# One halving of the key products on VectorE ahead of the identity matmuls, in a cached-attention decode kernel on Trainium2

## The chip, the cores and the metric

The kernel runs on one core of one Trainium2 chip. Its engines have an instruction stream each: TensorE (PE in the profile; PEld is its loading of the stationary operand), VectorE (DVE), ScalarE (ACT), GpSimd (POOL) and SyncE (SP), whose queue issues nearly all loads here. TensorE writes to PSUM; the other data lie in SBUF, 128 partitions wide. The metric is the device time of one execution in microseconds, the median of the runs.

## The reference

One token goes through a layer that mixes cached attention (32 heads, 65,536 cached keys and values of 128 numbers each, bf16) with a small gated feed-forward part.

```python
q = (x @ wq).reshape(B, Sq, H, Dh).transpose(0, 2, 1, 3)      # B = Sq = 1, H = 32, Dh = 128
scores = jnp.einsum("bhqd,bhkd->bhqk", q, k_cache) * (Dh ** -0.5)   # Sk = 65536
p = jax.nn.softmax(scores, axis=-1)
o = jnp.einsum("bhqk,bhkd->bhqd", p, v_cache)
a = o.transpose(0, 2, 1, 3).reshape(B, Sq, H * Dh) @ wo       # D = 512
b = (silu(x @ w_gate) * (x @ w_up)) @ w_down                  # F = 1792
g = sigmoid((x * gate_w).sum(-1, keepdims=True))
out = g * a + (1 - g) * b
```

The two caches are 32 x 65,536 x 128 bf16 each, some 537 MB; every byte is read once.

## The kernel before

A head's 65,536 keys are cut into CH = 4 chunks of 128 partitions x KPP = 128 keys, so there are N = 128 chunks in all. A chunk of keys, and one of values, fills one slot: 128 partitions x 16,384 bf16, 4 MB. There are SLOTS = 5 slots, used in turn by every tile that `slot()` hands out: the weights wq first, then key and value chunks in the order k0, k1, v0, k2, v1, k3, v2 and so on, and wo, the gate and up weights, and the down weights near the end. A load can be issued when the tile that had its slot five places earlier is no longer needed. All these loads go through SyncE's queue in that order (`load`, L111), so a load that waits for its slot holds those behind it. In steady state a value load of chunk n takes the slot of the keys of chunk n - 1, and a key load of chunk n that of the values of chunk n - 4.

The work on one chunk n goes in two halves of HK = 64 keys per partition:

- `products` (L163): VectorE multiplies the half's keys by q, in place. q lies in `q_bc`, the same on all partitions, and is read again for each of the 64 keys.
- `sums` (L178): TensorE adds up each key's 128 products. The identity is the stationary operand, so a matmul copies its moving operand, 64 keys x 8 of the 128 products, into one PSUM bank `S_ps`, and 16 matmuls in a row accumulate: 8 partial sums are left for each key.
- `gather` (L188): VectorE reduces these 8 to one score; after the second half ScalarE takes the exponential of all 128 scores (L193) into `P_sb` and adds up the row.
- `pv` (L216): TensorE multiplies with the values of the chunk before, 32 matmuls per chunk, 16 in each half, into `O_ps`, which gathers over a head's four chunks.

At a head's end `O_ps` is copied by ScalarE (L228), `diagonal` picks the diagonal blocks with tiny matmuls (L238), and ScalarE copies the result to `o_all` (L243). Before chunk 125 VectorE has three small operations (L251, L254, L346) that normalise the first 31 heads. At the end stand the projection of these heads (L320), the feed-forward part (L278 to L315), the values of the last two chunks and the last head's ending.

The program is written in this order, but the order on each engine is made by a scheduler when the program is built. On VectorE it came out as product, product, reduce, reduce for each chunk, where the second reduce of a chunk comes before the first product of the next. On TensorE it came out as 16 + 13 matmuls of L178, 16 of L216, the last 3 of L178, and 16 of L216. Engines wait for one another on semaphores; the waits that matter are those of L178 for the product (VectorE), of L188 for the last matmul of its half (TensorE), of L163 for the key load, and of the loads for the slot's last reader.

## Time and profile before

| what | value |
|---|---|
| median of 3 runs | 2546.85 us (2546.82 to 2547.63) |
| the profiled execution, its time | 2547.63 us |
| its span, first to last instruction | 2545.9 us |
| mean granted TensorE clock | 0.909 |
| HBM read | 1087.64 MB, 427 GB/s over the span |
| TensorE, identity matmuls (L178) | 4096, 437 ns each in the mean |
| TensorE, value matmuls (L216) | 4064, 379 ns each in the mean |
| VectorE, products (L163) | 254 long ones, 4421 ns each; 4 half as long, 2293 ns |
| VectorE, reduces (L188) | 256, 691 ns each |
| key load, issue to landing (median) | 37.9 us |
| value load, issue to landing (median) | 31.7 us |

The page shows busy times and shares by engine first, then the span in 40 slices of 63.6 us, where each digit is a busy share in tenths. A group's row reads: line, engine, operation, what it writes <- what it reads, count | total busy us, mean ns of one | idle time of the engine just before, and what ended it. The duration of a matmul is longer than its distance to the next one, since matmuls are pipelined. The granted clock is the share of TensorE's full clock that was allowed. In the timeline a row is a start, a length, the engine, line and operation, a count where several were merged, and in brackets the idle time before it with what ended it. A row of the waits says who waited for whom, with the total, the number of times and the longest.

### The profile page before, as it was taken

To read this page: it belongs to the slowest core of one execution; us is meant where nothing else is said; L and a number is where in the kernel's file an instruction comes from. 1 tells how busy PE (TensorE), PEld (TensorE's weight loads), DVE (VectorE), ACT (ScalarE), POOL (GpSimd) and SP (SyncE) were. 2 spreads that over 40 slices of the span, in tenths; PEclk is the share of its full clock that TensorE was granted. 3 is DMA by queue.
4 is the path that set the end of the run, shared out by engine and by line. 5 is a ranking of instruction groups with operands and counts; after the bars stand their busy time and mean duration, and the time that the engine had idled before them with its cause. 6 is when DMAs were issued, how large, how long until landed. Compare 5 with 4: busy or idle time off the path is not lost.

```text
span 2545.9 us, 19309 instructions
## 1 busy us (share of the span) xinstructions
PE 2085.1 (82%) x8741; PEld 811.0 (32%) x8742; DVE 1302.3 (51%) x535; ACT 82.1 (3%) x330; POOL 1.0 (0%) x8
## 2 busy tenths in 40 slices
PE   6888888788878877888888887878887888788878
PEld 2333333333333333333333332333333333233334
DVE  4445544554455455545554554455445545554552
ACT  1000000000000000000000000000000000000000
POOL 0000000000000000000000000000000000000000
PEclk8988898998998899999898899899899889999988
DMA  9999999999999999999999999999999999999998
GB/s 404 432 429 432 431 430 432 429 432 432 430 432 431 431 430 432 430 432 432 430 433 429 432 431 432 431 431 430 431 431 431 433 430 430 433 429 433 430 429 324
DMA packets 43416, 1088.88 MB, mean 428 GB/s; under 512 B 4291, under 2 KB 8390, under 8 KB 9670
## 3 DMA queue, kind: packets, MB, share of 16 engines
q1 hardware_dynamic: 43332, 1087.65, 99.6%
q8 instruction: 68, 1.11, 0.2%
q14 instruction: 14, 0.11, 0.0%
q10 hardware_dynamic: 2, 0.00, 0.0%
HBM read 1087.64 MB, written 0.00 MB: 427 GB/s over the span
## 4 chain that ended last, share of the span: by engine, by line
DMA 64%; PE 26%; DVE 9%; SPq 0%; issue 0%; ACT 0%; DVEq 0%
DMA slot<-in_A_k_cache_dram 63%; PE S_ps L178 13%; PE O_ps L216 12%; DVE slot L163 9%; DMA slot<-in_A_v_cache_dram 1%; SPq L263 0%; PE c_ps L206 0%; SPq L111 0%; PE c_ps L238 0%; ACT O_sb L228 0%; SPq L117 0%; PE tot_ps L247 0%; DVE out_sb L360 0%; SPq L98 0%; PE a_ps L320 0%
## 5 line engine op out<-in xcount | busy, mean ns | idle before, releaser
L178 PE MATMUL S_ps<-slot,ident 128*128 128x512 bf16 x4096 | 1127.5, 437 | 424.9 <-DVE slot L163 424.9
L163 DVE TENSOR_TENSOR slot<-slot,q_bc 128x8192 bf16<-128x8192 bf16 (+1 forms) x258 | 1121.7, 4388 | 251.8 <-DMA slot<-in_A_k_cache_dram 244.4
L216 PE MATMUL O_ps<-slot,P_sb 128*4 128x512 bf16 x4064 | 918.0, 379 | 1.2 <-DMA slot<-in_A_v_cache_dram 1.2
L178 PEld LDWEIGHTS <-ident 128*128 128x128 bf16 x4096 | 437.7, 109 | 1096.6 <-issue 772.7
L188 DVE TENSOR_REDUCE S_sb<-S_ps 128x64 f32<-128x512 f32 x256 | 176.9, 691 | 951.2 <-PE S_ps L178 951.2
L216 PEld LDWEIGHTS <-P_sb 128*4 128x4 bf16 x4064 | 324.2, 85 | 574.2 <-issue 108.3
L193 ACT ACTIVATE P_sb<-S_sb 128x128 bf16<-128x128 f32 x128 | 39.6, 309 | 2309.0 <-DVE S_sb L188 2309.0
L238 PE MATMUL c_ps<-pick,O_sb 4*128 4x1 f32 x256 | 33.5, 248 | 21.6 <-ACT O_sb L228 21.6
L238 PEld LDWEIGHTS c_ps<-pick,O_sb 4*128 4x128 f32 x256 | 30.8, 186 | 37.8 <-ACT O_sb L228 37.8
L193 ACT ACTIVATION_READ_ACCUMULATOR P_sb<-S_sb 128x1 f32 x128 | 23.9, 186 | 0.0
L228 ACT ACTIVATE O_sb<-O_ps 4x512 f32<-4x512 f32 x32 | 18.8, 586 | 87.0 <-PE O_ps L216 87.0
L137 PE MATMUL q_ps<-slot,X_bc 128*128 128x512 bf16 x31 | 8.5, 431 | 6.3 <-DMA slot<-in_A_wq_dram 6.3
L320 PE MATMUL a_ps<-slot,oT 128*1 128x512 bf16 x32 | 7.4, 385 | 0.3 <-DVE oT L356 0.3
L137 PEld LDWEIGHTS <-X_bc 128*128 128x128 bf16 x32 | 3.4, 108 | 11.2 <-issue 6.7
L278 PEld LDWEIGHTS <-slot 128*128 128x128 bf16 x112 | 6.8, 161 | 0.4 <-issue 0.4
L278 PE MATMUL gu_ps<-X_bc,slot 128*128 128x1 bf16 x112 | 6.9, 198 | 0.0
L286 DVE COPY gu_sb<-gu_ps 128x28 f32<-128x28 f32 x1 | 0.2, 186 | 12.9 <-PE gu_ps L278 12.9
L243 ACT ACTIVATE o_all<-c_ps 128x1 f32<-128x1 f32 x31 | 5.3, 171 | 35.3 <-PE c_ps L238 35.3
L297 PE MATMUL b_ps<-slot,hT 128*1 128x512 bf16 x14 | 4.8, 515 | 1.4 <-DVE hT L294 1.4
L144 ACT ACTIVATE q_bc<-q_ps 128x512 bf16<-128x512 f32 x8 | 4.8, 597 | 9.8 <-PE q_ps L137 9.8
L251 DVE TENSOR_REDUCE tot_10469<-tot_ps 128x1 f32<-128x4 f32 x1 | 0.2, 161 | 9.5 <-PE tot_ps L247 9.5
L320 PEld LDWEIGHTS <-oT 128*1 128x1 bf16 x32 | 2.6, 84 | 4.6 <-issue 0.4
(37 smaller groups left out, 19.2 us busy)
## 6 DMA issues: line engine op xcount, KB each, us to landing
slot<-in_A_k_cache_dram SPq DMA_DIRECT2D x127, 4096.0 KB, 37.9
slot<-in_A_v_cache_dram SPq DMA_DIRECT2D x127, 4096.0 KB, 31.7
slot<-in_A_k_cache_dram SPq DMA_DIRECT2D x4, 1024.0 KB, 11.2
slot<-in_A_wo_dram SPq DMA_DIRECT2D x1, 4096.0 KB, 29.7
slot<-in_A_wq_dram SPq DMA_DIRECT2D x1, 3072.0 KB, 21.2
slot<-in_A_v_cache_dram SPq DMA_DIRECT2D x1, 2048.0 KB, 25.8
slot<-in_B_w_gate_dram SPq DMA_DIRECT2D x1, 1792.0 KB
slot<-in_B_w_up_dram SPq DMA_DIRECT2D x1, 1792.0 KB, 14.4
```

Source lines behind the costliest of these rows:

```text
L137: nc.tensor.matmul(q_ps, lhsT=X_bc[:, t, :], rhs=wq_sb[:, t, g * QG : (g + 1) * QG], start=(t == 0), stop=(t == KT - 1),)
L144: nc.scalar.activation(out=q_bc[:, g * QG : (g + 1) * QG], in_=q_ps, func=ACT.Copy)
L163: nc.vector.tensor_tensor(out=w, in0=w, in1=q_rep, op=ALU.mult)
L178: nc.tensor.matmul(t, lhsT=ident, rhs=w[:, :, s * R : (s + 1) * R], start=(s == 0), stop=(s == steps - 1),)
L188: nc.vector.tensor_reduce(out=S_sb[n][:, i * HK : (i + 1) * HK], in_=S_ps.pop((n, i)), axis=AXIS.X, op=ALU.add)
L193: nc.scalar.activation(out=P_sb, in_=S_sb.pop(n), func=ACT.Exp, scale=scale, accum_out=rowsum[:, n : n + 1],)
L216: nc.tensor.matmul(O_ps[h], lhsT=probs[n][:, g * VB : (g + 1) * VB], rhs=kv["v", n][:, g * VB : (g + 1) * VB, :].rearrange("p a b -> p (a ...
L228: nc.scalar.activation(out=t, in_=O_ps.pop(h), func=ACT.Copy)
L238: nc.tensor.matmul(t, lhsT=O_sb[h][:, j * Dh : (j + 1) * Dh], rhs=pick[:, j : j + 1], start=(j == 0), stop=(j == VB - 1 and h < H - 1),)
L243: nc.scalar.activation(out=o_all[:, h : h + 1], in_=c_ps.pop(h), func=ACT.Copy)
L278: nc.tensor.matmul(gu_ps[:, w * FT + ft : w * FT + ft + 1], lhsT=gu[:, w * KT + t, bass.ds(ft, P, FT)], rhs=X_bc[:, t, 0:1], start=(t == 0 ...
L320: nc.tensor.matmul(a_ps, lhsT=oT[:, h : h + 1], rhs=wts["wo"][:, h, :], start=(h == 0), stop=(h == H - 1),)
```

## The change

One constant changes:

```diff
 VB = 4
 R = 8
-ADDS = 0
+ADDS = 1
```

It is read at two places. In `products` the loop over ADDS now runs once:

```python
            half = Dh
            for _ in range(ADDS):
                half //= 2
                nc.vector.tensor_tensor(
                    out=w[:, :, 0:half], in0=w[:, :, 0:half], in1=w[:, :, half : 2 * half],
                    op=ALU.add,
                )
```

After each product VectorE adds the second 64 products of each key to the first 64, in bf16 and in place (L167), an operation of 64 runs of 64 elements per partition; chunk 0, which is multiplied in four parts, has four adds of 32 runs. In `sums` the number of accumulating matmuls `steps = (Dh >> ADDS) // R` falls from 16 to 8 for each half. The PSUM tile, the reduce, the value matmuls, the head endings, the loads and the slots are as before.

On the engines the built program has another order. VectorE runs product, product, add, add, reduce, reduce for each chunk, the first add waiting for the first product and the second for the second. TensorE runs 8 matmuls of L178, 16 of L216, 8 of L178, 16 of L216; the first group of 8 waits for the first add, the second for the second. The order on SyncE's queue is the same.

## The prediction

> **What bounds the kernel now.** I read the page's first three parts, then the waits, then one chunk in the timeline. A chunk is one key slot and one value slot, 4096 KB each; there are 128.

> ```profile
> PE 2085.1 (82%) x8741; PEld 811.0 (32%) x8742; DVE 1302.3 (51%) x535; ACT 82.1 (3%) x330; POOL 1.0 (0%) x8
> ...
> DMA  9999999999999999999999999999999999999998
> GB/s 404 432 429 432 431 430 432 429 432 432 430 432 431 431 430 432 430 432 432 430 433 429 432 431 432 431 431 430 431 431 431 433 430 430 433 429 433 430 429 324
> ...
> q1 hardware_dynamic: 43332, 1087.65, 99.6%
> ```

> The DMA engines are full from the first slice to the last but one: the kernel streams at 431 GB/s. Two loads are 8.39 MB, 19.43 us at that rate, and in the timeline the first product of a chunk starts 19.43 us after that of the chunk before. That is the budget. What is left of it shows in the waits (total, times, longest):

> ```profile
> DVE S_sb L188 <- PE S_ps L178: 951.2, 234, 6.8
> ...
> PE S_ps L178 <- DVE slot L163: 424.9, 150, 8.8
> DVE slot L163 <- DMA slot<-in_A_k_cache_dram: 244.4, 127, 9.3
> ```

> VectorE waits for keys only 244.4/127 = 1.92 us a chunk, although it is half idle: the rest of its idle time is spent on TensorE (951.2 us), and TensorE's on VectorE (424.9 us). So behind the loads stands a second loop, the two engines taking turns, about 17.5 us long. The timeline of all engines, with the weight loads left out, shows the turns:

> ```profile
> 2397.34 8.76 DVE L163 TENSOR_TENSOR slot<-slot,q_bc 128x8192 bf16<-128x8192 bf16 x2 [2.60 <-DMA slot<-in_A_k_cache_dram]
> 2401.82 9.33 PE L178 MATMUL S_ps<-slot,ident 128*128 128x512 bf16 x29 [4.27 <-DVE slot L163]
> ...
> 2411.08 3.62 PE L216 MATMUL O_ps<-slot,P_sb 128*4 128x512 bf16 x16
> ...
> 2414.63 0.82 PE L178 MATMUL S_ps<-slot,ident 128*128 128x512 bf16 x3
> ...
> 2415.48 0.69 DVE L188 TENSOR_REDUCE S_sb<-S_ps 128x64 f32<-128x512 f32 x1 [6.34 <-PE S_ps L178]
> ...
> 2416.77 8.76 DVE L163 TENSOR_TENSOR slot<-slot,q_bc 128x8192 bf16<-128x8192 bf16 x2 [0.59 <-DMA slot<-in_A_k_cache_dram]
> ```

> TensorE starts after the first product, while the second runs. Its last S_ps matmuls stand behind 16 O_ps matmuls, the second reduce waits for them, and the next chunk's products are queued behind that reduce on VectorE. Here only 0.59 us were left before the next keys.

> **The change, part by part.** It removes 2048 of the 4096 identity matmuls (8 instead of 16 per half) and adds one VectorE add per product, 258 in all. Reduces, loads and O_ps matmuls keep their number and size. But the built program's order changes. VectorE now runs product, product, add, add, reduce, reduce. TensorE runs 8 S_ps, 16 O_ps, 8 S_ps, 16 O_ps. The first S_ps group waits for the first add, and so for both products; the second reduce waits for the second group of 8, behind 16 O_ps. So TensorE stands still while VectorE does two products and an add, and the first 4.34 us of overlap are lost.

> The add is in no row of before. The nearest rows, by shape:

> ```profile
> L163 DVE TENSOR_TENSOR slot<-slot,q_bc 128x8192 bf16<-128x8192 bf16 x254 | 1112.6, 4421 | 244.0 <-DMA slot<-in_A_k_cache_dram 244.0
> ...
> L163 DVE TENSOR_TENSOR slot<-slot,q_bc 128x4096 bf16<-128x4096 bf16 x4 | 9.2, 2293 | 7.8 <-ACT q_bc L144 7.3 <-DMA slot<-in_A_k_cache_dram 0.4
> ```

> The add writes 4096 results from two bf16 operands in runs of 64. Bounds: half a long product, 2.21 us; a whole one, 4.42 us, if the split rows cost half the rate. I take 2.29 us, the same instruction with as many results.

> The new loop, from a chunk's first product to the next one's, at full clock:
> - two products, 4.34 us from start to start (8.76 for the pair, 4.42 for one): 8.68
> - first add: 2.29 (the second runs beside TensorE, which needs it 5 us later)
> - VectorE's end to TensorE's first matmul: 2401.82 - 2397.34 - 4.42 = 0.06
> - 8 + 16 + 8 matmuls: from a group of 16, (3.62 - 0.38)/15 = 0.216 each, so 29 steps of 0.216 and two of 0.31 where the stationary changes (3 after 16 start 3.55 later): 6.88, and 0.41 from the last start to the reduce: 7.29
> - the reduce's start to the next product, where nothing else is awaited (2477.42 to 2478.03): 0.61

> Sum 18.93 us, 0.50 under the loads' 19.43. At full clock nothing would change. TensorE is not at full clock:

> ```profile
> 2397.34:2401.82 4.48, 0.21 (x2) 0.10 (x2) 4.48 (x2) 0.00 (x0) 0.00 (x0) 0.90 1.02 439
> 2401.82:2407.74 5.92, 5.92 (x14) 2.08 (x14) 4.28 (x1) 0.00 (x0) 0.00 (x0) 0.50 1.00 432
> 2407.74:2416.77 9.03, 9.03 (x42) 3.46 (x41) 1.39 (x3) 0.40 (x2) 0.00 (x0) 1.00 1.00 432
> ```

> In the new loop TensorE runs its last 16 matmuls (3.5 us) after the second reduce is released and then idles 0.61 + 11.03 (the first three terms) - 3.5 = 8.1 us, which always holds a window without work. So each chunk starts slow, for 2.6 us (start in the first quarter of a window) to 6.0 us (just after it). Half of that is lost: 1.3 to 3.0 us, a loop of 20.2 to 21.9. It is over 19.43 everywhere. Where it settles: six windows are 20.48 us, at which each chunk meets the grid at the same place; that needs 1.55 us lost, 3.1 us slow, inside the range; and a chunk that starts later in the window loses less and falls back towards that place. So I take 20.48. The loop holds there if its full-clock length is under about 19.2; above it the start slips out of the first quarter and the mean is near 21.3.

> [...]

> The sum of the span. First product of chunk 1: 36.0, set by its keys' landing; chunk 0's four products of 2.29 and four adds of half that run from 11.4 to before 30, hidden by that load. 126 loops of 20.48: 2580.5. The pause for the first 31 heads' sums: the timeline has 6.6 us from the reduce's start to the next product in place of 0.6, and the same order after: 6.0. The end: from the last chunk's first product before took 50.0, of which 1.2 was a wait for values; the last S_ps matmul now ends at about 16.1 instead of 12.9 after that product (11.03 + 16 at 0.216 + 1.6 for the clock): 52. Loads hide there, since the queue runs ahead. Sum 2674.5. The profiled execution's time is 1.7 above its span, the median of the runs 0.95: 2675.5.

> SP's queue: a value load waits for the key slot's last S_ps matmul, now 11.03 + 7.29 + 1.55 = 19.9 us after the first product instead of 16.1 (1011.97 to 1028.08); a key load for the value slot's last O_ps matmul, 3.6 later in both: 23.5 instead of 19.65. Loads now land 31.7 and 37.9 us after issue for 9.7 us of transfer, so 3.8 us later costs nothing; that cover only goes when two loads take longer than the loop, which the longer loop rules out.

> **Rivals.**
> - The loop slips the six-window place: an add of 2.6 us makes 19.24 and a mean of about 21.2; 36 + 126 x 21.2 + 58 = 2765. For: only 0.27 us of margin. Against: each term is a measured row.
> - The add runs at half rate, 4.42 us: 21.06 plus 2.15 (middle of 1.3 and 3.0) = 23.2; 36 + 126 x 23.2 + 60 = 3019. For: split rows that no row shows. Against: the product reads q_bc again for each of its 64 rows at the full rate.
> - Not slower: the clock recovers at once. It decides if the slow time is under 1.0 us a chunk, since half of that is the 0.50 spare. Then loads pace it as before: 2547 (the end grows by about 2 and is partly load-bound). For: the 18.93, and DMA 99.6% full. Against: 5.92 us at 0.50 after half the idle time.
> - The change doesn't do all that its words say: head endings are alike in both programs. Nothing of time hangs on it.

> **How the numbers follow.** Forecast 2675, own range 2665 to 2685: 0.70. Slipped loop, 2690 to 2830: 0.17. Half rate: 0.04. Something between the load bound and the forecast: 0.04. Not slower: 0.05, most of it within 0.2% (about 5 us, what a measurement here can tell from no change). The range 2655 to 2765 takes the forecast and most of the slipped loop. Slower 0.94, same 0.04, faster 0.02.

> **What would show it.** L167 at 2.29 us; VectorE's 244.4 us wait for keys near nothing; DMA share at 19.43/20.48 = 95%, some 409 GB/s; L178 x2048 with a mean near 0.379 + 0.255 x 7.3/16 = 0.495 us; products 20.48 us apart, with the granted clock low at each S_ps start. I am wrong if products stay 19.43 apart with full clock, or if the add is far from 2.29.

## The result and the profile after

The changed kernel takes 2678.8 us (median of 4 runs, 2677.44 to 2679.71) against 2546.99 us before: 1.0517 times as long, 95% interval 1.0498 to 1.0535. The profiled execution took 2677.44 us, its span is 2675.7 us.

The page of the changed kernel, its first three parts, as shown of before:

```profile
PE 1647.1 (62%) x6693; PEld 604.4 (23%) x6694; DVE 1856.0 (69%) x793; ACT 82.2 (3%) x330; POOL 1.0 (0%) x8
...
PEclk8888888888888888888888888888888888888877
DMA  9999999999999999999999999999999999999986
GB/s 406 430 431 432 431 420 407 410 412 411 405 412 410 412 405 413 409 410 407 414 410 408 407 410 412 410 406 406 422 400 413 415 409 407 414 410 407 409 367 242
...
q1 hardware_dynamic: 43332, 1087.65, 97.0%
```

TensorE lost 438 us of busy time, VectorE gained 554 us, and neither is full. The loads run at some 431 GB/s for the first 300 us, while they are still ahead of the engines, and then at some 409: they now wait for the engines. The DMA digits still say 9, so it is the GB/s row that tells. The waits (who <- whom: total, times, longest) say the same:

```profile
PE S_ps L178 <- DVE slot L167: 994.6, 129, 11.8
DVE S_sb L188 <- PE S_ps L178: 767.3, 255, 5.1
...
DVE slot L163 <- DMA slot<-in_A_k_cache_dram: 5.9, 1, 5.9
```

VectorE's wait for keys fell from 244.4 us to 5.9 us, once, at chunk 1. Instead the two engines wait for each other in every chunk. One chunk in the timeline of all engines (weight loads, ScalarE and SyncE left out):

```profile
1408.59 8.75 DVE L163 TENSOR_TENSOR slot<-slot,q_bc 128x8192 bf16<-128x8192 bf16 x2
...
1417.25 4.49 DVE L167 TENSOR_TENSOR slot<-slot 128x4096 bf16<-128x4096 bf16 x2
1419.59 3.45 PE L178 MATMUL S_ps<-slot,ident 128*128 128x512 bf16 x8 [8.10 <-DVE slot L167]
1422.97 3.62 PE L216 MATMUL O_ps<-slot,P_sb 128*4 128x512 bf16 x16
...
1426.52 1.90 PE L178 MATMUL S_ps<-slot,ident 128*128 128x512 bf16 x8
1428.35 3.62 PE L216 MATMUL O_ps<-slot,P_sb 128*4 128x512 bf16 x16
...
1428.46 0.69 DVE L188 TENSOR_REDUCE S_sb<-S_ps 128x64 f32<-128x512 f32 x1 [4.62 <-PE S_ps L178]
1429.07 8.75 DVE L163 TENSOR_TENSOR slot<-slot,q_bc 128x8192 bf16<-128x8192 bf16 x2
```

TensorE idles 8.10 us, until the first add is done. Its first 8 matmuls then take 3.38 us to the next group, where the second 8, at a granted clock of 1.00, take 1.83. The next product starts 1429.07 - 1408.59 = 20.48 us after the first. It does so in every chunk from the tenth to the 120th: the periods lie between 20.479 and 20.483 us, with a standard deviation of 0.001 us. Windows of the same chunk (length; busy PE, PEld, DVE, ACT, POOL; granted clock, DMA share, GB/s):

```profile
1419.59:1422.97 3.38, 3.38 (x8) 1.01 (x7) 2.15 (x1) 0.00 (x0) 0.00 (x0) 0.53 0.94 407
1422.97:1428.35 5.38, 5.38 (x25) 1.98 (x25) 0.69 (x1) 0.00 (x0) 0.00 (x0) 1.00 1.03 442
...
1408.59:1429.07 20.48, 12.38 (x50) 4.36 (x49) 14.45 (x8) 0.40 (x2) 0.00 (x0) 0.83 0.98 410
```

Of TensorE's groups only the first meets the half clock (0.53 in its window); from there to the end of the turn the clock is full (1.00). And the new add, by shape, beside the product with as many results:

```profile
L167 DVE TENSOR_TENSOR slot<-slot 128x4096 bf16<-128x4096 bf16 x254 | 569.6, 2283 | 0.0
...
L163 DVE TENSOR_TENSOR slot<-slot,q_bc 128x4096 bf16<-128x4096 bf16 x4 | 9.1, 2285 | 6.9 <-ACT q_bc L144 6.9
```

### The profile page after: what moved, and what is told of

Same layout as the page of the kernel before. It is cut to its first block, busy times and chain, and to the rows that moved or that the text cites. A ratio compares the mean times of both kernels' runs of the same rounds, so it can differ in the third digit from the quotient of the medians.

```text
span 2675.7 us, 15470 instructions
## 1 busy us (share of the span) xinstructions
PE 1647.1 (62%) x6693; PEld 604.4 (23%) x6694; DVE 1856.0 (69%) x793; ACT 82.2 (3%) x330; POOL 1.0 (0%) x8
## 3 DMA queue, kind: packets, MB, share of 16 engines
q1 hardware_dynamic: 43332, 1087.65, 97.0%
## 4 chain that ended last, share of the span: by engine, by line
DVE 52%; PE 43%; issue 3%; DMA 1%; SPq 0%; ACT 0%
DVE slot L163 42%; PE S_ps L178 25%; PE O_ps L216 17%; DVE slot L167 10%; DMA slot<-in_A_k_cache_dram 1%; PE a_ps L320 0%; PE gu_ps L278 0%; DVE S_sb L188 0%; PE b_ps L297 0%; PE c_ps L206 0%; SPq L111 0%; PE c_ps L238 0%; ACT O_sb L228 0%; PE tot_ps L247 0%; DVE out_sb L360 0%
## 5 line engine op out<-in xcount | busy, mean ns | idle before, releaser
L178 PE MATMUL S_ps<-slot,ident 128*128 128x512 bf16 x2048 | 687.6, 498 | 994.6 <-DVE slot L167 994.6
L163 DVE TENSOR_TENSOR slot<-slot,q_bc 128x8192 bf16<-128x8192 bf16 (+1 forms) x258 | 1120.3, 4383 | 12.8 <-ACT q_bc L144 6.9
L216 PE MATMUL O_ps<-slot,P_sb 128*4 128x512 bf16 x4064 | 918.9, 379 | 0.0
L188 DVE TENSOR_REDUCE S_sb<-S_ps 128x64 f32<-128x512 f32 x256 | 177.0, 692 | 767.3 <-PE S_ps L178 767.3
L167 DVE TENSOR_TENSOR slot<-slot 128x4096 bf16<-128x4096 bf16 (+1 forms) x258 | 574.5, 2267 | 0.1
L178 PEld LDWEIGHTS <-ident 128*128 128x128 bf16 x2048 | 230.5, 117 | 1395.9 <-issue 1304.4
L216 PEld LDWEIGHTS <-P_sb 128*4 128x4 bf16 x4064 | 324.3, 85 | 611.3 <-issue 146.1
L238 PE MATMUL c_ps<-pick,O_sb 4*128 4x1 f32 x256 | 33.5, 248 | 21.6 <-ACT O_sb L228 21.6
L228 ACT ACTIVATE O_sb<-O_ps 4x512 f32<-4x512 f32 x32 | 18.8, 586 | 85.8 <-PE O_ps L216 85.8
L286 DVE COPY gu_sb<-gu_ps 128x28 f32<-128x28 f32 x1 | 0.2, 186 | 12.9 <-PE gu_ps L278 12.9
L278 PEld LDWEIGHTS <-slot 128*128 128x128 bf16 x112 | 6.8, 161 | 0.4 <-issue 0.4
L278 PE MATMUL gu_ps<-X_bc,slot 128*128 128x1 bf16 x112 | 6.9, 198 | 0.0
L144 ACT ACTIVATE q_bc<-q_ps 128x512 bf16<-128x512 f32 x8 | 4.8, 597 | 9.9 <-PE q_ps L137 9.9
## 6 DMA issues: line engine op xcount, KB each, us to landing
slot<-in_A_k_cache_dram SPq DMA_DIRECT2D x127, 4096.0 KB, 20.3
slot<-in_A_v_cache_dram SPq DMA_DIRECT2D x127, 4096.0 KB, 13.8
```

What stands on the lines that cost most here:

```text
L163: nc.vector.tensor_tensor(out=w, in0=w, in1=q_rep, op=ALU.mult)
L167: nc.vector.tensor_tensor(out=w[:, :, 0:half], in0=w[:, :, 0:half], in1=w[:, :, half : 2 * half], op=ALU.add,)
L178: nc.tensor.matmul(t, lhsT=ident, rhs=w[:, :, s * R : (s + 1) * R], start=(s == 0), stop=(s == steps - 1),)
L188: nc.vector.tensor_reduce(out=S_sb[n][:, i * HK : (i + 1) * HK], in_=S_ps.pop((n, i)), axis=AXIS.X, op=ALU.add)
L216: nc.tensor.matmul(O_ps[h], lhsT=probs[n][:, g * VB : (g + 1) * VB], rhs=kv["v", n][:, g * VB : (g + 1) * VB, :].rearrange("p a b -> p (a ...
L228: nc.scalar.activation(out=t, in_=O_ps.pop(h), func=ACT.Copy)
```

## The experiments

All start from the changed kernel. A single run has no interval; where one is given, it comes from runs of that kernel and of the one before in turn.

### Only the order: the first add ahead of the second product

`behind` sets the order of issue on VectorE and adds no wait.

```diff
+    last_add = {}
...
-            nc.vector.tensor_tensor(out=w, in0=w, in1=q_rep, op=ALU.mult)
+            prod = nc.vector.tensor_tensor(out=w, in0=w, in1=q_rep, op=ALU.mult)
+            if n in last_add:
+                behind(prod, last_add[n])
...
-                nc.vector.tensor_tensor(
+                last_add[n] = nc.vector.tensor_tensor(
```

> The changed kernel with one order edge: a chunk's second product stands behind its first add, so VectorE runs product, add, product, reduce, add, reduce. Same work. Theory (the loss is the lost overlap in the order): TensorE starts 6.8 us after a chunk's first product instead of 11.0, the turn of both engines is 17 to 18.5 us, the loads' 19.43 sets the pace again, and the time is 2545 to 2550. Rival (the adds' 575 us of extra VectorE work cost the time): unchanged work, so 2670 to 2680. Rival (later release of slots starves the loads): release moves back with the order, so this run alone does not tell it from the theory.

Measured: 2545.44 us, 0.9993 of before (0.9984 to 1.0002), with every add still there. The timeline of a chunk (lines are shifted by the edit: L173 the products, L179 the adds, L190 the identity matmuls, L200 the reduces, L228 the value matmuls):

```profile
1400.18 4.43 DVE L173 TENSOR_TENSOR slot<-slot,q_bc 128x8192 bf16<-128x8192 bf16 x1 [2.07 <-DMA slot<-in_A_k_cache_dram]
...
1404.64 2.29 DVE L179 TENSOR_TENSOR slot<-slot 128x4096 bf16<-128x4096 bf16 x1
1406.85 4.42 DVE L173 TENSOR_TENSOR slot<-slot,q_bc 128x8192 bf16<-128x8192 bf16 x1
1406.99 3.47 PE L190 MATMUL S_ps<-slot,ident 128*128 128x512 bf16 x8 [6.06 <-DVE slot L179]
1410.39 3.62 PE L228 MATMUL O_ps<-slot,P_sb 128*4 128x512 bf16 x16
...
1411.79 2.28 DVE L179 TENSOR_TENSOR slot<-slot 128x4096 bf16<-128x4096 bf16 x1
...
1414.12 1.89 PE L190 MATMUL S_ps<-slot,ident 128*128 128x512 bf16 x8
...
1416.05 0.69 DVE L200 TENSOR_REDUCE S_sb<-S_ps 128x64 f32<-128x512 f32 x1 [1.98 <-PE S_ps L190]
```

TensorE starts 6.81 us after the first product, as expected, and its slow group (3.40 us, at a granted clock of 0.52) lies beside the second product. The second group starts at 1414.12, when the second add is done (1411.79 + 2.28); TensorE itself was free some 0.1 to 0.2 us before. VectorE waits for keys again, 2.07 us here. Without that wait the turn is some 16.5 us long (from 1400.18 to the second reduce at 1416.05, and 0.61 more to the next product), under the 17 to 18.5 us that were expected. So the extra VectorE work costs nothing by itself here; the place of the first add does.

### Only the clock: TensorE kept busy while it would stand still

```diff
-    ps_s = ctx.enter_context(tc.tile_pool(name="ps_s", bufs=3, space=bass.MemoryType.PSUM))
+    ps_s = ctx.enter_context(tc.tile_pool(name="ps_s", bufs=2, space=bass.MemoryType.PSUM))
...
+    def keep_warm():
+        for j in range(31):
+            ins = nc.tensor.matmul(w_ps, lhsT=ident, rhs=q_bc[:, 0:512], start=True, stop=True)
+            tc.keep_in_program_order(ins)
...
                 pv(n - 1, i)
+                if i == HALVES - 1:
+                    keep_warm()
```

> The changed kernel plus 31 identity matmuls per chunk into a scratch bank, behind the chunk's value matmuls, in the time in which TensorE stood still; their result is not read. S_ps has two banks instead of three to make room. VectorE's order and the real work are unchanged. Theory (the half clock at each chunk's start is what lifts the loop over the loads' pace): clock 1.0 throughout, loop 18.9 by itself, loads set 19.43, time 2545 to 2555. Rival (the order and the adds alone make the loop longer than the loads): still 20.48 a chunk or more, 2675 or over. Rival (more TensorE work can only cost): over 2680.

Measured: 2550.51 us, 1.0013 of before (1.0004 to 1.0022): 31 useless matmuls more in each chunk, and 128 us less than the changed kernel. The order is that of the changed kernel. First the products in VectorE's timeline from the start, then a window in the middle:

```profile
56.75 8.75 DVE L163 TENSOR_TENSOR slot<-slot,q_bc 128x8192 bf16<-128x8192 bf16 x2
...
75.67 8.75 DVE L163 TENSOR_TENSOR slot<-slot,q_bc 128x8192 bf16<-128x8192 bf16 x2
...
94.58 8.75 DVE L163 TENSOR_TENSOR slot<-slot,q_bc 128x8192 bf16<-128x8192 bf16 x2
```

```profile
1414.42:1419.79 5.37, 5.37 (x25) 1.95 (x24) 2.75 (x2) 0.00 (x0) 0.00 (x0) 1.00 0.98 418
```

At 56.75, 75.67 and 94.58 keys had landed already and nothing but the engines' turn counted: it is 18.92 and 18.91 us long, against 18.93 in the prediction's sum. Once it has caught up with the loads, most products start some 19.43 us apart. The clock, expected at 1.0 throughout, was 0.989 in the mean: it still dropped now and then. Both parts are thus needed for the loss: the order makes the turn long, the half clock lifts it over the loads.

### The place where the turn settles: other lengths of the turn

The edit of the run with 4 matmuls; the other three have 9, 10 and 12 in that place.

```diff
-        for s in range(steps):
+        count = steps if i == 0 else 4
+        for s in range(count):
             nc.tensor.matmul(
-                t, lhsT=ident, rhs=w[:, :, s * R : (s + 1) * R],
-                start=(s == 0), stop=(s == steps - 1),
+                t, lhsT=ident, rhs=w[:, :, s % steps * R : (s % steps + 1) * R],
+                start=(s == 0), stop=(s == count - 1),
             )
```

> The changed kernel with only 4 of the 8 identity matmuls in each chunk's second half (the scores of that half leave out half of their products). These 4 lie on the turn of the engines at full clock, 0.86 us a chunk. Theory (the turn locks to six windows of the clock's grid, 20.48 us): the period stays at 20.48 and the time at 2670 to 2677. Rival (the time is the sum of the parts, clock loss constant): 126 x 0.86 = 109 us less, about 2570.

> The changed kernel with one identity matmul more in each chunk's second half (it adds one group of products a second time, so that half's scores are changed). Full-clock turn 18.92 + 0.22 = 19.14 us, just under the 19.2 at which the lock was taken to end. Theory: 20.48 a chunk if the margin is as worked out, time 2675 to 2682; at 21.0 to 21.3, 2745 to 2780, if the clock needs a little more work in a window to return than was read. Rival (sum of parts): 126 x 0.22 = 27 us more than the changed kernel, about 2705.

> As the run with one more, but two more identity matmuls in the second half. Full-clock turn 19.35 us, past the lock. Theory: the start slips through the clock's grid, mean period 21.3 to 21.6, unequal periods, time 2780 to 2820. Rival (sum of parts): 54 us more than the changed kernel, about 2733.

> Four more identity matmuls in the second half. Full-clock turn 19.78 us. Theory: mean period 21.8 to 22.2, time 2845 to 2895. Rival (sum of parts): 109 us more than the changed kernel, about 2788.

| matmuls in the second half | full-clock turn, worked out | mean period, chunks 11 to 121 | time | sum of parts |
|---|---|---|---|---|
| 4 | 18.06 us | 20.48 us | 2677.95 us | 2570 us |
| 8 (the changed kernel) | 18.92 | 20.48 | 2678.8 | 2678.8 |
| 9 | 19.14 | 20.48 | 2679.69 | 2705 |
| 10 | 19.35 | 21.34 | 2782.69 | 2733 |
| 12 | 19.78 | 21.85 | 2844.26 | 2788 |

Taking half of the second group away saves nothing; one matmul more costs nothing; the second one more costs 103 us at once. A sum of parts gives none of the four. The periods are as expected in all four; two of the times lie just outside what was written down, 2677.95 us with 4 matmuls (at most 2677) and 2844.26 us with 12 (at least 2845). With 4 matmuls TensorE's timeline shows where the saved 0.86 us went (L179 identity, L217 value matmuls):

```profile
1419.20 3.57 PE L179 MATMUL S_ps<-slot,ident 128*128 128x512 bf16 x8 [8.11 <-DVE slot L167]
1422.70 4.36 PE L217 MATMUL O_ps<-slot,P_sb 128*4 128x512 bf16 x16
1426.99 1.04 PE L179 MATMUL S_ps<-slot,ident 128*128 128x512 bf16 x4
```

The 16 value matmuls behind the slow group take 4.36 us instead of 3.62: the half clock lasts longer, and takes the saving back. The granted clock is 0.50 from 1419.20 to 1423.00, past the start of these matmuls, where in the changed kernel it is 1.00 from their start on; in the mean of the run it is 0.751 instead of 0.833. With 10 matmuls the products in VectorE's timeline are no longer evenly spaced:

```profile
1400.91 8.75 DVE L163 TENSOR_TENSOR slot<-slot,q_bc 128x8192 bf16<-128x8192 bf16 x2
...
1421.89 8.75 DVE L163 TENSOR_TENSOR slot<-slot,q_bc 128x8192 bf16<-128x8192 bf16 x2
...
1442.62 8.75 DVE L163 TENSOR_TENSOR slot<-slot,q_bc 128x8192 bf16<-128x8192 bf16 x2
...
1464.87 8.75 DVE L163 TENSOR_TENSOR slot<-slot,q_bc 128x8192 bf16<-128x8192 bf16 x2
```

20.98, 20.73 and 22.25 us: the start no longer meets the clock's grid at the same place in each chunk, as the prediction's slipped-loop rival had it. But it does not drift either. These three and a fourth period of 21.38 us repeat up to chunk 121, and the four together are 85.33 us, 25 steps of 3.413 us; with 12 matmuls five periods repeat, 109.23 us together, 32 steps. So these two kernels are tied to the grid as well, over several chunks instead of one.

### Fewer bytes

Both engines' orders were pinned to those of the changed kernel's chunks; the edit that counts:

```diff
+        if which == "v" and n < N - 1:
+            pieces = [HK]
...
-                rhs=kv["v", n][:, g * VB : (g + 1) * VB, :].rearrange("p a b -> p (a b)"),
+                rhs=kv["v", n][:, g % G * VB : (g % G + 1) * VB, :].rearrange("p a b -> p (a b)"),
```

> The changed kernel, its engine orders pinned, with only the first half of each value chunk loaded (the second half's value matmuls use the first half's values again). Loads fall from 8.39 to 6.29 MB a chunk, 14.6 us. Theory (the turn of the engines sets the pace, loads do not): period 20.48 still, time 2660 to 2680. Rival (late slots or starved loads set the pace): the period falls towards 15 to 18 us, time 1950 to 2350.

Measured: 2663.45 us, the period 20.48 us again, with a standard deviation of 0.001 us. The page's GB/s row and the median times to landing:

```profile
GB/s 403 338 300 295 321 316 300 294 321 315 300 293 323 315 300 292 320 319 300 292 320 318 300 292 319 320 300 292 317 321 300 292 317 320 302 291 316 321 302 241
...
slot<-in_A_k_cache_dram SPq DMA_DIRECT2D x127, 4096.0 KB, 13.4
slot<-in_A_v_cache_dram SPq DMA_DIRECT2D x128, 2048.0 KB, 7.2
```

With a quarter of the bytes gone the pace is the same, so neither the loads nor the slots set it. The 15 us less come from the pinned order near the end. It has no pause before chunk 125 (20.48 instead of 26.15 us). And after the last chunk's first product 42.8 us are left instead of 52.4: TensorE does the projection and the gate and up matmuls, 13.6 us in the changed kernel, before the last identity matmuls and no longer behind them. The chain of work that ended last holds no load there in either kernel.

### A version for the end

On top of the first experiment's order:

```diff
-        if n == N - 2:
-            load_tail_weights()
         load("v", n, [KPP] if n < N - 1 else tail_pieces)
+        if n == N - 2:
+            load_tail_weights()
...
+    for i in range(HALVES):
+        pv(N - 2, i)
     for hh in range(H - 1):
         project(hh)
     ffn()
-    for i in range(HALVES):
-        pv(N - 2, i)
```

> The add-first version (e1_add_first), and at the end the last but one value chunk is loaded ahead of the tail weights and its value matmuls run before the projection, so the 7 us of them no longer stand behind the feed-forward part. Work is the same. If the end after the last load is what is left above the loads' pace: 2538 to 2543, below both kernels. If the chain at the end only trades places (feed-forward part now last, waiting for its weights): 2543 to 2549.

Measured: 2544.55 us, 0.9989 of before (0.9980 to 0.9998). It is 2.75 us under the kernel before, 0.1%, with an interval that only just leaves out no change. That is the second of the two outcomes written down, 2543 to 2549 us: the feed-forward part took the place of the value matmuls as the last work before the final head. It doesn't wait for its weights there, as had been written: the chain of work that ended last holds no load after the last keys, and the feed-forward part follows the projection on TensorE.

## Why the prediction was right

- The bound. "A second loop stands behind the loads": shown. In the changed kernel VectorE waits for keys once, and with fewer bytes nothing changes.
- The order as the cause. Shown by the first experiment: with the adds kept and TensorE's start back from 11.0 to 6.8 us, the loss is gone.
- The add's price. Taken 2.29 us, measured 2.283. In its runs of 64 the add took no longer than the product with as many results, 2.285; the half-rate rival, 4.42, falls.
- The full-clock turn. Sum 18.93 us, measured 18.92 and 18.91 with TensorE kept busy. The claim that at full clock nothing would change came out at 1.0013 of before, with the clock at 0.989.
- The clock's surcharge. Taken 1.55 us, measured 20.48 - 18.92 = 1.56.
- Where it settles. The starts of the first chunks are 20.85, 20.66, 20.60, 20.56, 20.52 us apart, and by the tenth 20.48: the difference shrinks, as a stable place asks. The end of the one-chunk lock, put at a full-clock turn of about 19.2 us, lies between 19.14 and 19.35; the mean beyond it, put near 21.3, is 21.34 and 21.85. The margin was thin: with a turn 0.43 us longer the kernel takes 2782.69 us, so a term too small by that much would have made the slipped loop true.
- The sum. Chunk 1 began at 35.60 us (taken 36.0); the 126 periods of 20.48 make 2580.5, and the approach at the start 0.8, the pause 5.7 (taken 6.0) and the last two periods 0.8 come on top, which puts chunk 127 at 2623.35; the end took 52.4 (taken 52). Span 2675.7 against 2674.5. The terms left out are the two of 0.8.
- What would show it. L178's mean was expected at 495 ns and is 498; GB/s 409 as expected. The DMA share of the load queue was expected at 95% and is 97.0%. The same packets took longer: per DMA engine 97.0% of 2675.7 us, 2595, after 99.6% of 2545.9, 2536. Why is not shown; the bytes per second are the safer row.
- SP's queue. Loads land 13.8 (values) and 20.3 us (keys) after issue instead of 31.7 and 37.9. The time to landing shrank by some 18 us, and the keys still land early enough: VectorE waits for them only at chunk 1.

What is not shown is what the clock's grid is. That the clock record changes in steps of 3.413 us was read from the trace (in before, all but the last of its 216 stretches are whole numbers of steps long); that the period is six such steps, for three lengths of the turn, is measured. What the prediction has of the clock's return was fitted to the trace of before: each of its 107 returns to full clock follows a step with matmuls in at least 76.6% of its time, and no step after which the clock stayed half had more than 74.8%. In steady state the runs fit it: the step ahead of a return is filled to 94% with 8 matmuls in the second half and to 81% with 9; with 10, one of the four in turn is filled to 75.5%, and the clock stays half for another step. The 40% under which the prediction has the clock drop is not a sharp line: no step with under 41% left the clock of before full, but 22 of its 108 drops followed steps with more than 42%, most of them at heads' ends. The prediction's sum does not rest on that number: 8.10 us of idle time are longer than two steps, and of the changed kernel's 129 drops 95 followed an empty step and 32 one with at most 36%, nearly all of these with the small matmuls of a head's end. Behind the last chunk neither reading holds. In the changed kernel the clock dropped after a step full of the gate and up matmuls (L278, 112 in 6.83 us), and stayed half after one full of 128 short matmuls (L206, 165 ns each, 3.42 us).

## What to carry to other kernels

When two engines take turns, count the turn from start to start with the order that the built program has, at the clock that it will have after its own idle time, and compare it with the loads' pace: here, with loads of 19.43 us, 18.92 us at full clock was hidden and 20.48 was not. TensorE, with work taken off it, stood still for 8.10 us a chunk, and the group behind that pause ran at a granted clock of 0.53. And moving work to another engine was free here or not by where in the turn it lay, at the same length: 2545.44 us with the first add ahead of the second product, 2678.8 with it behind. Look at the order first: one edge between an add and a product was worth 5%.

## What the runs showed of the hardware that was not expected

That a whole kernel can lock to the clock's grid so exactly: for turns of 18.06 to 19.14 us at full clock, as worked out, the period was 20.48 us with a standard deviation of 0.001 us over 110 chunks, in four kernels, and 0.22 us more made it 21.34 in the mean, in a pattern of four chunks that is locked in its turn. In such a place the time did not answer to a saving of 0.86 us, and the mean granted clock does not tell the time either: it was 0.751 with 4 matmuls and 0.833 with 8, at the same time, and 0.823 in the add-first version, which runs at the loads' pace.
